# Fills, two factor products, four stores and three GpSimd steps moved between engines in a fused attention and feed-forward kernel

## The chip, the cores and the metric

One core of one Trainium2 chip. The metric is the device time of one execution in microseconds. The time before is the median of three runs.

## The reference

The inputs are q, k and v of 4 batches, 8 heads, 768 positions and 64 columns, and three arrays of a feed-forward layer. Attention comes first; every query sees the 8 first keys and the 96 last ones (abbreviated here):

```python
scores = scale * np.matmul(q, k.transpose(0, 1, 3, 2))
keep = is_global | is_local
dist = np.where(is_global & ~is_local, float(n_local), np.abs(rel))
scores = np.where(keep, scores - slopes[:, None, None] * dist, -1e9)
a = softmax(scores)                      # over the keys
x = (a @ v) as 3072 rows of 512
h = x @ w_in                             # 3072 x 1024
solu = h * softmax(h)                    # over the 1024
ln = (solu - mean(solu)) / sqrt(var(solu) + 1e-6) * g_ln
out = ln @ w_out                         # 3072 x 512, float32
```

## The kernel before, in words

**Tiling.** The program handles the batches one after the other, and within a batch four pairs of heads. For each pair it loads q and k (L477), casts them to 16 bits on VectorE, ScalarE or GpSimd (`x`, L264, L266, L268), turns them on TensorE (L741; for batch 3 by DMA, L776) and copies the result to `qT` and `kT`. Scores of a pair stand in two groups of key blocks (L892); ScalarE takes their exponential into `eb` (L900). In batch 0 the distance bias is added by a matmul (L878); in batches 1 to 3 `eb` is multiplied by a ready factor `fb` instead (L909, the "factor product": one instruction on VectorE, four quarters on GpSimd). Sums (L973), the logarithm (L989, L998), its spread to all rows (L1028), its exponential `rr` (L1037), the product with v (L1072, with a small VectorE read `tick`, L1082, between its halves) and the scaling to `xT` (L1097) end the attention of half a batch.

**The feed-forward part** has 24 row tiles of 128. A tile takes a first product (L1133), an exponential `ef` on ScalarE (L1140), VectorE's product `uu` (L1143), a sum of squares (L1150 or L1154), a turn of `uu` (L1169, from tile 5 on by DMA, L1159), small statistics (L1189 to L1198), a second product with the centred weights (L1215), the scaling `osb` (L1226, L1229) and a store (L1233). The first tile to be handled is tile 2.

**Weights.** `w_out` is multiplied by g (the weighting, L644 to L651, on three engines), TensorE forms the mean over the rows (L658), and VectorE subtracts it in eight steps (the centring, L662). The mean stays in one PSUM bank while the centring reads it; the first second product, that of tile 2, writes the same bank.

**The order.** Every piece of work is a numbered `step` with the engines that may do it. Three tables written into the program decide: `ORDER` is the order in which all steps are issued, so each engine and each queue executes its own in this order; `SLOTS` gives the buffers; `ENGS` the engine where a step has a choice. `WARM` names places in ORDER at which spare matmuls are put. An instruction waits only for what it needs, but everything behind it on its engine waits as well. SyncE issues nearly all DMAs; two stores at the end are issued by ScalarE.

**The steps that the change and the prediction touch:**

- 6, `c_slr` (L372 to L374): eight memsets of `slr`, which `constants_far` (L385) reads on VectorE. On GpSimd it stands between `c_spread` (L361) and a cast of v.
- 359 and 362: the factor products of batch 1, second group, pairs 0 and 1, both on VectorE. 359 stands between a cast of v and `uu` of tile 2 and reads the exponential of step 358, done at 25.52 us. 362 stands behind 350, the product of the first group's pair 1, ahead of an `xT` product, a copy, another `xT` product and the centring.
- on GpSimd from 27.5 us: casts of q of batch 1, pairs 2 and 3; one weighting step (159, two halves); casts of k, pairs 2 (300) and 3 (313); two casts of v; two kg steps; two weighting steps.
- 302 and 315: copies of the turned k of pairs 2 and 3, on ScalarE and on VectorE (L264, L266).
- 836, 824, 830 and 907: the stores of tiles 5, 3, 4 and 9. Their `osb` are written by VectorE (5, 3, 4) and ScalarE (9).
- 602, 51, 662 and 637 on GpSimd: the kg of batch 3, pair 0 (L523), its `vgz` (L515), the cast of its v of pair 2 and the cast of its k of pair 3 (L268). They stand behind 683, the factor product of batch 3, second group, pair 0.
- 519: the first scores of batch 2's second group. They write the bank pair that the first product of tile 4 used, which is free when `uu` of tile 4 has been formed.

Of the kernel before, what the change touches and what calls it, by code (L numbers as in the profile page):

```python
# [60 lines left out]
"""  # L61
SLOTS = """
# [10 lines left out]
"""  # L73
ENGS = """
# [1206 lines left out]
```

## Time and profile before

| what | value |
|---|---|
| median of three runs | 152.86 us (152.83 to 153.1) |
| the profiled execution | 152.65 us, its span 150.9 us |
| TensorE busy | 142.4 us, 94% |
| VectorE busy | 117.9 us, 78% |
| ScalarE busy | 122.1 us, 81% |
| GpSimd busy | 69.9 us, 46% |
| DMA queue of SyncE | 76120 packets, 97.5% of 16 engines' span |
| DMA queue of ScalarE | 288 packets, 0.9% |

The span is the time from the first to the last instruction of one profiled execution; 1.75 us of that execution's own time lie around it. Busy times of TensorE count pipelined matmuls with modelled ends, so small waits can hide in them. In the rows PE is TensorE, DVE VectorE, ACT ScalarE, POOL GpSimd and SP SyncE; L12 is line 12 of the program, and the lines named above are the lines of the rows. A row of a timeline gives the start in us from the span's start, the length in us, the engine, the line, the operation, out<-in with the shapes, and how many instructions are merged; in brackets stand the idle time of the engine before it and what ended it by the semaphores.

### The profile page before, as it was taken

Reading aid. Unit: us, or ns where it says so; the run is one execution under the profiler, and the core shown is the slowest. Engines: PE = TensorE matmul, PEld = TensorE weight load, DVE = VectorE, ACT = ScalarE, POOL = GpSimd, SP = SyncE. Lnnn points to the kernel's source line nnn. Section 1 sums busy time; section 2 is a strip of 40 time slices with the busy share of each in tenths; the row PEclk is TensorE's granted clock in tenths of the full one; section 3 lists DMA queues with packets and bytes.
Section 4 is the critical chain, followed back from the end, with each engine's and each line's share of the span. In section 5 each row is a group of like instructions: output and inputs, shape, how many; then the busy total and the mean of one; then the engine's idle time right before and its main releaser. Section 6 shows DMA issues by size and latency. Waiting matters only on the chain.

```text
span 150.9 us, 4802 instructions
## 1 busy us (share of the span) xinstructions
PE 142.4 (94%) x1870; PEld 76.7 (51%) x1870; DVE 117.9 (78%) x241; ACT 122.1 (81%) x209; POOL 69.9 (46%) x192
## 2 busy tenths in 40 slices
PE   5979799999998999999999999999999999999991
PEld 2536556466554566744454645444446644444450
DVE  6939897998999997989899966697785874898200
ACT  3949899899999789899997987978895776874641
POOL 6784447559899769735922240498130000110000
PEclk9999999999999999999999999999999999999999
DMA  4999999999999999999999999998999946488743
GB/s 140 367 307 342 300 382 337 362 337 401 309 295 182 247 323 220 240 216 250 241 160 235 260 161 260 162 221 159 223 212 260 216 125 128 81 245 208 231 152 139
DMA packets 76430, 36.35 MB, mean 241 GB/s; under 512 B 65456, under 2 KB 71928, under 8 KB 76408
## 3 DMA queue, kind: packets, MB, share of 16 engines
q1 hardware_dynamic: 76120, 35.54, 97.5%
q10 hardware_dynamic: 288, 0.52, 0.9%
q8 instruction: 14, 0.23, 0.6%
q14 instruction: 8, 0.07, 0.1%
HBM read 23.15 MB, written 6.29 MB: 195 GB/s over the span
## 4 chain that ended last, share of the span: by engine, by line
PE 72%; ACT 9%; DMA 7%; SPq 5%; DVE 4%; issue 1%; DVEq 0%; ACTq 0%
PE acc L1215 28%; PE acc L1133 23%; PE acc L1072 6%; DMA vt<-in_v_dram 4%; DMA x<-in_q_dram 3%; PE acc L892 3%; ACT eb L900 3%; PE acc L1028 3%; PE acc L973 2%; PE acc L741 2%; SPq L477 2%; ACT ef L1140 2%; DVE x L266 2%; PE acc L1062 1%; SPq L499 1%
## 5 line engine op out<-in xcount | busy, mean ns | idle before, releaser
L1215 PE MATMUL acc<-gw_out_sb,late 128*128 128x512 f16 (+1 forms) x200 | 44.3, 371 | 0.4 <-DMA vt<-in_v_dram 0.4
L1133 PE MATMUL acc<-w_in_sb,xT 128*128 128x512 f16 x192 | 44.7, 379 | 0.0
L1143 DVE SCALAR_TENSOR_TENSOR uu<-ef,acc 128x1024 f16<-128x1024 f16 x24 | 29.2, 1216 | 8.6 <-ACT ef L1140 8.4
L900 ACT ACTIVATE eb<-acc 128x896 f16<-128x896 f32 (+1 forms) x32 | 29.1, 955 | 1.5 <-PE acc L892 1.4
L1140 ACT ACTIVATE ef<-acc 128x1024 f16<-128x1024 f32 x24 | 24.7, 1030 | 6.5 <-PE acc L1133 6.5
L1215 PEld LDWEIGHTS <-late 128*128 128x128 f16 x200 | 18.9, 98 | 21.5 <-issue 1.3
L1133 PEld LDWEIGHTS <-xT 128*128 128x128 f16 x192 | 17.8, 98 | 21.4 <-issue 1.4
L268 POOL CAST x<-x 128x384 f16<-128x384 f32 (+1 forms) x32 | 17.9, 586 | 12.3 <-DMA x<-in_q_dram 6.2
L1097 DVE TENSOR_TENSOR xT<-acc,rr 128x384 f16<-128x384 f32 x32 | 16.3, 551 | 3.9 <-ACT rr L1037 1.5
L1072 PE MATMUL acc<-eb,v 64*64 64x160 f16 (+4 forms) x448 | 16.0, 221 | 0.6 <-DVE xT L1097 0.3
L1150 ACT ACTIVATE sqa<-uu 128x1024 f16<-128x1024 f16 x15 | 15.9, 1063 | 0.0
L909 POOL TENSOR_TENSOR eb<-eb,fb 128x240 f16<-128x240 f16 (+1 forms) x20 | 12.5, 656 | 6.1 <-ACT eb L900 6.1
L1072 PEld LDWEIGHTS <-v 64*64 64x64 f16 x448 | 12.9, 106 | 4.5 <-issue 3.4
L1037 ACT ACTIVATE rr<-acc 128x768 f32<-128x768 f32 x16 | 12.6, 811 | 2.8 <-PE acc L1028 1.9
L268 POOL CAST v<-v 128x384 f16<-128x384 f32 (+3 forms) x23 | 10.9, 492 | 7.2 <-DMA v<-in_v_dram 6.3
L909 DVE TENSOR_TENSOR eb<-eb,fb 128x896 f16<-128x896 f16 (+1 forms) x19 | 13.3, 727 | 1.1 <-ACT eb L900 1.1
L741 PE MATMUL acc<-ident,x 128*128 128x128 f16 x144 | 11.1, 220 | 1.5 <-ACT x L264 1.0
L892 PE MATMUL acc<-qT,kT 64*64 64x160 f16 (+2 forms) x384 | 11.8, 227 | 0.0
L1154 DVE SCALAR_TENSOR_TENSOR sqv<-uu 128x1024 f16<-128x1024 f16 x9 | 11.3, 1251 | 0.1
L741 PEld LDWEIGHTS <-x 128*128 128x128 f16 x144 | 8.5, 98 | 4.8 <-ACT x L264 1.4
L1226 ACT ACTIVATE x<-acc,rstd 128x512 f32<-128x512 f32 (+1 forms) x9 | 5.8, 640 | 6.2 <-PE acc L1215 6.2
L1062 PE MATMUL acc<-eg,vgz 64*64 64x384 f16 x64 | 10.7, 324 | 0.0
(120 smaller groups left out, 206.1 us busy)
## 6 DMA issues: line engine op xcount, KB each, us to landing
x<-in_q_dram SPq DMA_DIRECT2D x16, 384.0 KB, 5.8
x<-in_k_dram SPq DMA_DIRECT2D x16, 384.0 KB, 5.1
out_dram<-osb SPq DMA_DIRECT2D x12, 256.0 KB, 4.9
v<-in_v_dram SPq DMA_DIRECT2D x12, 192.0 KB, 4.5
out_dram<-x SPq DMA_DIRECT2D x9, 256.0 KB, 2.3
late<-in_moe_w_in_dram SPq DMA_DIRECT2D x4, 512.0 KB, 6.6
w_out<-in_moe_w_out_dram SPq DMA_DIRECT2D x4, 512.0 KB, 6.0
v<-in_v_dram SPq DMA_DIRECT2D x12, 160.0 KB, 4.7
```

The source lines that it names most:

```text
L268: nc.gpsimd.tensor_copy(out=out, in_=in_)
L741: nc.tensor.transpose(out=pt[:, ts(j, P)], in_=a[:, j, ts(pp, P)], identity=ident)
L892: nc.tensor.matmul(out=sc[o : o + 64, par, col : col + n], lhsT=kk[r, BLK * c : BLK * c + BLK], rhs=qq[r, g0 : g0 + n], start=fresh, stop= ...
L900: ex["fn"] = (lambda ex=ex, qk=qk, gw=gw: nc.scalar.activation(out=eb[at(qk, "eb")][:, :, 0:gw], in_=big(qk)[:, :, 0:gw], func=AF.Exp, sca ...
L909: (nc.gpsimd if fx["at"] == "POOL" else nc.vector).tensor_tensor(out=e[:, :, y], in0=e[:, :, y], in1=fb[:, p, :, y], op=ALU.mult)
L1072: nc.tensor.matmul(out=o_[64 * h : 64 * h + 64, gl : gl + m], lhsT=vv[r, v_at(vi, h, c), pair, :], rhs=view(eb[at(e_own[b, gi, pair], "eb" ...
L1097: nc.vector.tensor_tensor(out=xT[at(xt_own[b], "xT")][:, p, q0:q1], in0=one(av, d)[:, 0:w], in1=rr[at(re, "rr")][:, d, 0:w], op=ALU.mult)
L1133: nc.tensor.matmul(out=ph()[:, ts(fh, 512)], lhsT=xT[at(xt_own[b], "xT")][:, j, ts(t % NA, P)], rhs=w_in_sb[:, j, ts(fh, 512)], start=((j, ...
L1140: ex["fn"] = lambda g1=g1, t=t, ph=ph: nc.scalar.activation(out=ef[at(g1, "ef")], in_=ph(), func=AF.Exp, accum_out=s0[:, t : t + 1])
L1143: u["fn"] = lambda u=u, g1=g1, t=t, ph=ph: nc.vector.scalar_tensor_tensor(out=uu[at(u, "uu")], in0=ef[at(g1, "ef")], scalar=USC, in1=ph(), ...
L1150: nc.scalar.activation(out=sqs_["ACT"], in_=uu[at(u, "uu")], func=AF.Square, scale=float(D_FF) ** 0.5, accum_out=s2[:, t : t + 1])
L1215: nc.tensor.matmul(out=one(g2)[:, 0:wd], lhsT=uT[at(el_o, "uT")][:, c, :], rhs=gw_out_sb[:, c, sl_], start=(c == 0), stop=(c == NFC - 1))
```

## The change

It changes three lines of code and the four tables. The tables are long lists of numbers; what follows from them is this:

- `c_slr` runs on VectorE, behind the copy of q that ends at 8.46 us and ahead of the next cast.
- Step 359 runs on GpSimd, in four quarters, behind the cast of q of pair 3 and ahead of the weighting step 159.
- Step 362 stays on VectorE and stands behind the eight centring steps and `uu` of tile 5, ahead of a copy of q.
- Stores may now be issued by ScalarE for every tile; four are. 836 and 824 (tiles 5 and 3) stand behind the exponential `ef` of tile 6 and ahead of an `rr` exponential (L1037); 830 (tile 4) stands behind a sum of squares and ahead of an `osb`; 907 (tile 9) behind `rstd` (L1198) and ahead of an `osb`. They leave SyncE's list at four places, in front of loads and transposes.
- On GpSimd 602, 51 and 662, and with them 637, stand ahead of 683.

All else keeps its place on its engine: TensorE's list with the spare matmuls, SyncE's other DMAs, and all buffers are the same.

```diff
     def constants_slr():
         for h in range(H):
-            nc.gpsimd.memset(slr[:, h : h + 1], -slopes[h] * NL)
+            nc.vector.memset(slr[:, h : h + 1], -slopes[h] * NL)
...
-    slr_st = step("POOL", 270, -59000, [], constants_slr, name="c_slr")
+    slr_st = step("DVE", 560, -59000, [], constants_slr, name="c_slr")
...
-                        wd * 1.31, tg + 2500, [ou], eng=("SP",) if x < 20 else ("SP", "ACT"), name="store", iss=420)
+                        wd * 1.31, tg + 2500, [ou], eng=("SP", "ACT"), name="store", iss=420)
...
 ORDER = """
-126 86 12 11 271 2 13 17 16 10 15 66 14 18 0 20 73 36 3 75 7 1 4 88 68 69 89 22 53 55 56 90 8 70 38 79 81
+126 271 2 52 86 12 11 18 66 13 73 0 36 3 53 17 20 7 16 38 10 15 14 1 79 4 88 28 68 115 22 60 75 117 69 89
...
 WARM = """
-25:0:16 30:2:4 37:3:2 48:5:3 118:7:4
+34:0:16 43:2:4 49:3:2 59:5:3 126:7:4
```

## Rows read from the trace of the kernel before

**Rows 1.** Windows: us, busy us of PE, PEld, DVE, ACT, POOL, clock, DMA share, GB/s.

```profile
40.00:52.00 12.00, 11.53 (x109) 5.51 (x111) 12.00 (x20) 10.88 (x21) 11.04 (x23) 1.00 1.11 246
60.00:120.00 60.00, 60.00 (x875) 31.59 (x875) 49.17 (x91) 50.87 (x88) 25.29 (x58) 1.00 1.13 215
```

**Rows 2.** Timeline of TensorE around 50 us.

```profile
48.17 1.89 PE L1215 MATMUL acc<-gw_out_sb,late 128*128 128x512 f16 x8 [0.43 <-DMA vt<-in_v_dram]
...
51.92 0.22 PE L878 MATMUL acc<-bw,identb 64*64 64x64 f16 x2
```

**Rows 3.** Timeline of VectorE, 28 to 52 us.

```profile
28.04 0.92 DVE L909 TENSOR_TENSOR eb<-eb,fb 128x896 f16<-128x896 f16 x1
28.89 1.21 DVE L1143 SCALAR_TENSOR_TENSOR uu<-ef,acc 128x1024 f16<-128x1024 f16 x1
...
30.26 0.56 DVE L266 CAST x<-x 128x768 f16<-128x768 f32 x1 [0.15 <-DMA x<-in_q_dram]
...
35.30 0.96 DVE L266 COPY kT<-acc 128x768 f16<-128x768 f16 x1
...
39.84 1.49 DVE L909 TENSOR_TENSOR eb<-eb,fb 128x960 f16<-128x960 f16 x2
40.40 0.92 DVE L909 TENSOR_TENSOR eb<-eb,fb 128x896 f16<-128x896 f16 x1
41.25 0.54 DVE L1097 TENSOR_TENSOR xT<-acc,rr 128x384 f16<-128x384 f32 x1
...
42.78 5.34 DVE L662 SCALAR_TENSOR_TENSOR gw_out_sb<-w_out,g,acc 128x512 f16<-128x512 f32 x8
48.04 1.21 DVE L1143 SCALAR_TENSOR_TENSOR uu<-ef,acc 128x1024 f16<-128x1024 f16 x1
...
50.65 1.21 DVE L1143 SCALAR_TENSOR_TENSOR uu<-ef,acc 128x1024 f16<-128x1024 f16 x1
```

**Rows 4.** Timeline of VectorE, start of the kernel.

```profile
1.40 0.77 DVE L305 MEMSET sl<- 64x1 f32 x8
...
7.50 0.96 DVE L266 COPY qT<-acc 128x768 f16<-128x768 f16 x1
11.01 0.72 DVE L266 CAST x<-x 128x768 f16<-128x768 f32 x1 [2.55 <-DMA x<-in_q_dram]
```

**Rows 5.** Timeline of ScalarE, tile 2's exponential, its last part.

```profile
28.65 0.19 ACT L1140 ACTIVATION_READ_ACCUMULATOR ef<-acc 128x1 f32 x1
```

**Rows 6.** Timeline of GpSimd, casts, weighting and factor products.

```profile
28.90 0.96 POOL L268 CAST x<-x 128x384 f16<-128x384 f32 x2 [0.41 <-DMA x<-in_q_dram]
31.66 1.18 POOL L647 TENSOR_TENSOR gw_out_sb<-w_out,g 128x256 f16<-128x256 f32 x2 [1.80 <-DMA w_out<-in_moe_w_out_dram]
32.78 2.01 POOL L268 CAST x<-x 128x384 f16<-128x384 f32 x4
...
58.52 2.74 POOL L909 TENSOR_TENSOR eb<-eb,fb 128x240 f16<-128x240 f16 x4
...
96.54 2.31 POOL L909 TENSOR_TENSOR eb<-eb,fb 128x224 f16<-128x224 f16 x4 [5.89 <-ACT eb L900]
```

**Rows 7.** Timeline of VectorE, a cast and four factor products.

```profile
59.70 1.06 DVE L266 CAST x<-x 128x768 f16<-128x768 f32 x1
...
106.33 2.30 DVE L909 TENSOR_TENSOR eb<-eb,fb 128x896 f16<-128x896 f16 x4 [0.53 <-ACT eb L900]
```

**Rows 8.** Timeline of TensorE, the transposes of k of batch 1, pair 3.

```profile
34.42 0.77 PE L741 MATMUL acc<-ident,x 128*128 128x128 f16 x6
```

**Rows 9.** Timelines of ScalarE and of SyncE, a gap and two stores.

```profile
82.68 0.81 ACT L1037 ACTIVATE rr<-acc 128x768 f32<-128x768 f32 x1 [0.77 <-PE acc L1028]
...
143.37 0.37 ACTq L1233 DMA_DIRECT2D out_dram<-x  x1
...
81.59 1.40 SPq L1233 DMA_DIRECT2D out_dram<-osb  x1
```

**Rows 10.** Chain that ended last: start, us, what.

```profile
114.55 0.56 PE acc L973 x24
```

80 rows, old and new, of tables (ENGS, ORDER, SLOTS) are left out of this document.

## The prediction

> **What bounds the kernel now.** I read the windows by stage first. From 60 to 120 us TensorE is busy for 60.00 of 60 us; from 40 to 52 us it is VectorE that has no idle time (12.00 of 12), with TensorE at 11.53 [rows 1]. The granted clock is 1.00 in all of these stretches, so the clock is no part of the argument. What can be won therefore lies ahead of 52 us, and whatever delay TensorE still has at 52 us goes to the end unreduced, because nothing idles behind it.
>
> Next the timeline of TensorE around 50 us [rows 2]. The first output product (tile 2, L1215) starts at 48.17 us after 0.43 us of idle time; the bank that it writes is the one the centring reads, and VectorE's eight centring steps, begun at 42.78 us, end at 42.78 + 5.34 = 48.12 us [rows 3]. That is the wait the change aims at. But four starts later, at 51.92 us, the scores of batch 2 (L878) begin in the bank pair that VectorE's product `uu` of tile 4 gives back, and that product ends at 50.65 + 1.21 = 51.86 us [rows 2, 3]. So TensorE and VectorE arrive at 52 us together: a faster start at 48.17 us alone brings nothing unless tile 4's `uu` is earlier too. The reader is to see that VectorE's row of steps from 35 to 52 us is the path that decides, and its total work, not its order.
>
> **The change part by part.**
>
> *Fills of slopes to VectorE.* Eight memsets, as long there as the eight of `sl`, 0.77 us. They come behind the copy that ends at 7.50 + 0.96 = 8.46 us, and VectorE's next step starts at 11.01 us after 2.55 us of waiting for a load [rows 4]. They fit: cost nothing. If that load came 1.8 us earlier they would cost up to 0.77 us.
>
> *The product of batch 1, second group, pair 0, to GpSimd.* On VectorE it takes 0.92 us from 28.04 us. The next step there, `uu` of tile 2, starts at 28.89 us, but the exponential that it reads ends at 28.65 + 0.19 = 28.84 us, and the cast behind it waits until 30.26 us for a load [rows 3, 5]. So VectorE gains 0.05 us at most: it idles instead. GpSimd is free from 28.90 + 0.96 = 29.86 us and waits 1.80 us, until 31.66 us, for the output weights [rows 6]. Four quarters of this width cost 2.31 us there undisturbed; the product beginning at 58.52 us took 2.74 us, and beside it VectorE's cast of `x` took 1.06 us where the same cast took 0.56 us at 30.26 us [rows 3, 6, 7]. The new product has that very cast, at 30.26 us, beside it.
>
> The Trainium skill (SBUF — State Buffer, section SBUF: two separate sides) says that a GpSimd instruction and a VectorE one that needs the shared port pair exclude each other for the whole instruction. By it the cast would hold up GpSimd for its full 0.56 us, 2.87 us in all; the pair of lengthened rows agrees in kind.
>
> So GpSimd is through at 29.86 + 2.31 = 32.17 us or 29.86 + 2.74 = 32.60 us, 0.5 to 0.9 us behind the start of the weighting at 31.66 us. Behind it stand two weighting halves and then the casts of batch 1's keys, pairs 2 and 3. These take 2.01 us for four where two take 0.96 us, so about 0.1 us of waiting inside is swallowed. TensorE turns these keys at 34.42 us, and its six transposes take 0.77 us because it already waits for the second half of the last cast [rows 6, 8]; VectorE copies the result at 35.30 us [rows 3], first step of its unbroken row. Nothing covers this delay: the bounds are +0.3 us (part of it swallowed at each hand-over) and +0.9 us. The rows give 2.74 us for a product of 240 columns a quarter; for 224 columns 2.56 us, 0.7 us late, less the 0.1 us: I take **+0.6 us**.
>
> *The product of pair 1 behind the centring.* It goes from ahead of the centring (0.92 us at 40.40 us) to behind `uu` of tile 5 (48.04 us), ahead of tile 4's `uu` [rows 3]. The centring and the product at 48.17 us come earlier by its slot, 41.25 − 40.40 = 0.85 us (its successor, an `xT` product, starts at 41.25 us [rows 3]), but the work ahead of 51.86 us is the same. What can change is its length: four such products back to back take 2.30 us [rows 7], 0.57 each, so it loses up to 0.28 us if GpSimd is quiet at the new place, and nothing if GpSimd casts there too; its old neighbour could be lengthened by as much in its stead. Bounds −0.3 and +0.3 us; GpSimd has casts at both places, half of the gain: **−0.15 us**.
>
> *Four stores begun by ScalarE* (tiles 5 and 3 behind an exponential, 4 and 9 further on). An issue there took 0.37 us, at the end of the kernel. Two of them stand in the 0.77 us before the exponential of the spread logarithms at 82.68 us [rows 9]; 0.74 us fits. The other two are alone in front of waits. Cost nothing, as long as they are that short. SyncE's later loads and transposes move up by the slots left; TensorE waits for none of them there [rows 1], so no gain.
>
> *Three (with the last cast of keys: four) ready steps of GpSimd ahead of a product.* GpSimd idles 5.89 us before that product at 96.54 us [rows 6]. A kg step, two halves of `vgz` and two casts are under 4 us, so they fit. Should the cast of keys wait for its buffer, the product behind it waits with it; its readers, the sums at 114.55 us [rows 10], are 18 us later. Nothing either way.
>
> **Sum:** 0 − 0.05 + 0.6 − 0.15 + 0 + 0 = +0.4 us. The profiled execution took 152.65 us, 0.21 us below the median of the three runs, 152.86 us; so 152.65 + 0.4 = 153.05 us for such an execution and 152.86 + 0.4 = 153.26, say 153.3 us, for a median. 0.2% of this kernel is 0.31 us, about what a measurement can tell from no change; the forecast lies just beyond it.
>
> **The rivals.**
>
> *It evens out.* GpSimd is undisturbed (+0.3 us) and the moved product sheds its 0.28 us: 152.86 us, anything within 0.31 us. For it: the cast at 30.26 us overlaps only one quarter of four. Against it: the lengthened pair of rows. 0.29.
>
> *Faster: the wait at 48.17 us goes.* TensorE starts tile 2's product 0.43 us earlier, which counts from the point where tile 4's `uu` ends at least 0.43 us earlier too: the moved product alone at its new place (−0.28 us), its neighbour at 39.84 us not lengthened either, and GpSimd's new product hidden in the 1.80 us of waiting as far as the key casts' readers can see. Price −0.43 us: 152.4 us. For it: VectorE's products were lengthened twice before (0.92 us at 28.04 and 40.40 us [rows 3]) and one of the two leaves it. Against it: 2.31 us do not fit into 1.80 us. 0.23.
>
> *Slower by the stores.* SyncE's issue of the same kind took 1.40 us at 81.59 us, when the DMA engines were full [rows 9]. Should ScalarE be held as long, the two stores cost 2.8 − 0.77 = 2.0 us in front of 82.68 us, more than the later gaps of ScalarE return; TensorE's tiles behind wait for these exponentials, about +1.5 us, 154.4 us. Against it: ScalarE has a queue of its own that holds nothing. 0.04.
>
> **How the numbers follow.** Forecast (GpSimd's delay reaches 52 us) 0.44, evens out 0.29, faster 0.23, stores 0.04. Slower by over 0.2%: 0.44 + 0.04 = 0.48; within: 0.29; faster: 0.23. Of the forecast the bounds +0.9 and +0.3 − 0.3 give 152.9 to 154.1 us; the range 152.5 to 153.9 us leaves out the dearest tail, the stores and the lower half of the faster case. The forecast's own range is 153.1 to 153.9 us.
>
> **What would show it.** Right: on GpSimd the product at 29.9 us taking 2.3 to 2.9 us, the weighting behind it at 32.2 to 32.6 us, VectorE's copy of keys (35.30 us before) at 35.6 to 36.2 us; VectorE idle ahead of tile 2's `uu`; TensorE's first output product without its 0.43 us of waiting, and a new wait at the scores of batch 2 near 52.3 us; no idle TensorE behind. Wrong: the scores of batch 2 earlier than 51.9 us, or the weighting still at 31.7 us, or a stall of ScalarE at a store.

## The result and the profile after

| | kernel before | changed kernel | ratio, 95% interval |
|---|---|---|---|
| first measurement | 153.00 us (152.83 to 153.18) | 154.97 us (154.26 to 156.92) | 1.0104 [1.0062, 1.0147] |
| second measurement, another chip | 153.7 us | 156.19 us (155.27 to 158.76) | 1.0162 [1.0130, 1.0195] |

The forecast was 153.3 us, within 152.5 to 153.9 us: slower, as it came, but the loss is 1.0 to 1.6% where 0.3% was expected. Each set of runs has its own runs of the kernel before on the same chip; the chips of the later sets scatter more than the first. A ratio leaves disturbed executions out, so it isn't always that of the two medians.

The profile shown is that of the changed kernel in the second measurement: 155.27 us, span 153.4 us. In the kernels of the runs the tables are one to three lines longer, so here every line stands two higher: L1235 is the store, L911 the factor product, L880 the scores' first line.

Page of the changed kernel: the head, the DMA queues, and the costliest group.

```profile
span 153.4 us, 4804 instructions
...
PE 142.8 (93%) x1870; PEld 76.8 (50%) x1870; DVE 117.0 (76%) x248; ACT 122.4 (80%) x209; POOL 72.8 (47%) x188
...
q1 hardware_dynamic: 75544, 34.49, 95.0%
q10 hardware_dynamic: 864, 1.57, 2.9%
...
L1135 PE MATMUL acc<-w_in_sb,xT 128*128 128x512 f16 x192 | 44.4, 379 | 1.4 <-ACT osb L1228 1.4
```

TensorE's work is the same 142 us; what is new is 1.4 us of idle time before a first product, ended by ScalarE's `osb`. The stages show where (windows, columns as in [rows 1]).

```profile
40.00:52.00 12.00, 11.52 (x119) 5.85 (x117) 12.00 (x21) 11.70 (x21) 10.46 (x23) 1.00 0.98 228
60.00:90.00 30.00, 29.96 (x442) 16.42 (x440) 27.54 (x51) 27.47 (x48) 14.34 (x32) 1.00 1.17 216
90.00:100.00 10.00, 8.62 (x96) 4.29 (x94) 5.45 (x11) 7.27 (x14) 6.28 (x15) 1.00 1.21 219
```

From 60 to 120 us TensorE was never idle before [rows 1]; now it loses 1.38 us between 90 and 100 us. The clock is 1.00 throughout. The timelines of ScalarE, TensorE and SyncE give the cause.

```profile
88.29 0.69 ACT L1228 ACTIVATE osb<-acc,rstd 128x512 f32<-128x512 f32 x1 [0.51 <-PE acc L1217]
...
93.87 0.21 ACT L1200 ACTIVATE rstd<-vb 128x3 f32<-128x3 f32 x1
96.02 0.34 ACTq L1235 DMA_DIRECT2D out_dram<-osb  x1
96.48 0.69 ACT L1228 ACTIVATE osb<-acc,rstd 128x512 f32<-128x512 f32 x1 [2.40 <-DMA late<-uu]
...
97.22 1.89 PE L1135 MATMUL acc<-w_in_sb,xT 128*128 128x512 f16 x8 [1.38 <-ACT osb L1228]
...
82.21 3.36 SPq L778 DMA_TRANSPOSE qT<-x  x1
...
90.09 3.73 SPq L1161 DMA_TRANSPOSE late<-uu  x1
```

ScalarE has finished `rstd` at 94.08 us. Next in its list is the store of tile 9, whose `osb` (the row at 88.29 us) has been ready since 88.98 us. It begins only at 96.02 us, 1.94 us later, and its issue then takes 0.34 us. What ended the wait is a DMA of SyncE, the transpose of a `uu` begun at 90.09 us, with which the store has no data in common; by the trace it landed at 96.00 us. In this program all DMAs, of whichever queue, share eight completion semaphores in turn (the counters that tell that a transfer has landed; the trace has 143 DMAs on eight of them, 17 or 18 on each), and the program makes a DMA that comes to use one wait until the transfer that used it before has landed. The store and that transpose have the same one. Everything behind the store on ScalarE waits with it: `osb` of the next tile, whose PSUM bank TensorE's first product at 97.22 us needs. Of the 2.40 us of idle time in front of this `osb`, 0.94 us were there before, in a wait for TensorE:

```profile
93.94 0.69 ACT L1226 ACTIVATE osb<-acc,rstd 128x512 f32<-128x512 f32 x1 [0.94 <-PE acc L1215]
```

So the store adds about 1.5 us, and TensorE loses 1.38 us.

The other half of the loss lies earlier (VectorE, GpSimd and TensorE; to be held against [rows 2, 3, 6]).

```profile
30.23 2.62 POOL L911 TENSOR_TENSOR eb<-eb,fb 128x224 f16<-128x224 f16 x4
32.81 1.18 POOL L649 TENSOR_TENSOR gw_out_sb<-w_out,g 128x256 f16<-128x256 f32 x2
...
36.30 0.96 DVE L268 COPY kT<-acc 128x768 f16<-128x768 f16 x1 [0.70 <-PE acc L743]
...
43.49 5.34 DVE L664 SCALAR_TENSOR_TENSOR gw_out_sb<-w_out,g,acc 128x512 f16<-128x512 f32 x8
48.75 1.21 DVE L1145 SCALAR_TENSOR_TENSOR uu<-ef,acc 128x1024 f16<-128x1024 f16 x1
...
49.89 0.61 DVE L911 TENSOR_TENSOR eb<-eb,fb 128x896 f16<-128x896 f16 x1
...
51.82 1.21 DVE L1145 SCALAR_TENSOR_TENSOR uu<-ef,acc 128x1024 f16<-128x1024 f16 x1
...
48.88 1.89 PE L1217 MATMUL acc<-gw_out_sb,late 128*128 128x512 f16 x8 [0.41 <-DMA vt<-in_v_dram]
53.09 0.22 PE L880 MATMUL acc<-bw,identb 64*64 64x64 f16 x2 [0.31 <-DVE uu L1145]
```

By these times the copy of keys is 1.0 us late, `uu` of tile 4 and the scores of batch 2 1.2 us. About 0.4 us of that is not the change's: GpSimd's cast of q ahead of the product already ends at 30.27 us and not at 29.86 us, and in the profiles of the runs it ends anywhere between 29.8 and 31.3 us, with the product behind it or without. From that cast's end to the copy it is 6.03 us against 5.44 us. The first output product still waits (0.41 us; 0.43 us before), and the scores have a wait of 0.31 us that they didn't have.

### The profile page after: what moved, and what is told of

It is laid out like the page before. It is cut to its first block, busy times and chain, and to the rows that moved or that the text cites. A ratio compares the mean times of both kernels' runs of the same rounds, so it can differ in the third digit from the quotient of the medians.

```text
span 154.9 us, 4804 instructions
## 1 busy us (share of the span) xinstructions
PE 143.2 (92%) x1870; PEld 76.9 (50%) x1870; DVE 116.6 (75%) x248; ACT 122.1 (79%) x209; POOL 71.4 (46%) x188
## 4 chain that ended last, share of the span: by engine, by line
PE 55%; DVE 9%; DMA 4%; ACT 2%; issue 1%; ACTq 0%; DVEq 0%
PE acc L1215 24%; PE acc L1133 18%; DMA late<-uu 4%; PE acc L1072 4%; DVE gw_out_sb L662 3%; PE acc L892 2%; PE acc L973 2%; DVE xT L1097 2%; PE acc L1028 1%; PE acc L741 1%; DVE uu L1143 1%; PE acc L1062 1%; DVE sqv L1154 1%; DVE l L998 1%; PE acc L946 1%
## 5 line engine op out<-in xcount | busy, mean ns | idle before, releaser
L909 POOL TENSOR_TENSOR eb<-eb,fb 128x240 f16<-128x240 f16 (+1 forms) x24 | 15.2, 663 | 1.5 <-ACT eb L900 1.5
L1037 ACT ACTIVATE rr<-acc 128x768 f32<-128x768 f32 x16 | 12.6, 811 | 2.8 <-PE acc L1028 1.9
L909 DVE TENSOR_TENSOR eb<-eb,fb 128x896 f16<-128x896 f16 (+1 forms) x18 | 12.5, 714 | 0.8 <-ACT eb L900 0.8
```

The source lines that it names most:

```text
L909: (nc.gpsimd if fx["at"] == "POOL" else nc.vector).tensor_tensor(out=e[:, :, y], in0=e[:, :, y], in1=fb[:, p, :, y], op=ALU.mult)
```

## The experiments

Edits of the tables are shown as the lists of the engines they touch, by step numbers, with "..." for what is left out between. "Order only" is the base of most.

**Parts of the change: stores, the rest, and the interleaving.** The changed kernel again:

```diff
 (the changed kernel, nothing edited)
```

> The changed kernel once more, for a profile to set the others against. Theory A (the stores on ScalarE): ScalarE stands idle for about 2 us in front of the store of tile 9, waiting for an earlier transfer to land, and TensorE waits for 1 to 2 us at a first product behind it; 154.3 to 155.3 us. Theory B (the product on GpSimd): the scores of batch 2 start at 52.5 us or later where they started at 51.9 us; the same time. Theory C (the interleaving of the lists, which sets the semaphores): TensorE is already 0.5 us late at 26 us, as in the first profile of this kernel; the same time.

156.19 us, ratio 1.0162 [1.0130, 1.0195]: above the expected time. That chip's kernel before is above too, but the ratio is also larger than the first one. ScalarE's idle time (2.40 us) and the late scores (53.09 us) are both there.

The four stores back with SyncE:

```diff
-ScalarE: 841 836 824 537 ... 857 830 906 ... 862 907 876
+ScalarE: 841 537 ... 857 906 ... 862 876
-SyncE: 609 616 606 858 635 642 844 632 625 619 851 612
+SyncE: 609 836 616 824 606 858 635 642 907 844 632 625 619 851 830 612
```

> The changed kernel with the four stores back in SyncE's list, all else as changed. Theory A: nearly all of the loss goes, 153.0 to 153.6 us (what is left is the 0.4 us of the forecast), and TensorE has no wait over 0.5 us between 90 and 100 us. Theory B: only the part behind 90 us goes, 154.0 to 154.6 us. Theory C: little goes, about 154.5 us.

154.52 us, 1.0064 [1.0037, 1.0091]. Only the stores on ScalarE:

```diff
-VectorE: 90 6 62 ... 193 773 ... 350 265 ... 815 362 445
+VectorE: 90 62 ... 193 359 773 ... 350 362 265 ... 815 445
-GpSimd: 9 119 ... 320 359 159 ... 602 51 662 637 683 628 615 641
+GpSimd: 9 6 119 ... 320 159 ... 683 637 602 628 662 615 51 641
```

> The changed kernel with the fills, both factor products and the GpSimd steps back at their old engines and places; the four stores stay on ScalarE. Theory A: 154.0 to 154.8 us, with ScalarE idle for about 2 us in front of the store of tile 9. Theory B: 153.0 to 153.3 us. Theory C: 153.6 us, and the scores of batch 2 start late although GpSimd has no product there.

154.93 us, 1.0065 [1.0031, 1.0098], with 2.20 us of idle time of ScalarE and 1.18 us of TensorE. "Order only" takes both edits:

```diff
-ScalarE: 841 836 824 537 ... 857 830 906 ... 862 907 876
+ScalarE: 841 537 ... 857 906 ... 862 876
-SyncE: 609 616 606 858 635 642 844 632 625 619 851 612
+SyncE: 609 836 616 824 606 858 635 642 907 844 632 625 619 851 830 612
-VectorE: 90 6 62 ... 193 773 ... 350 265 ... 815 362 445
+VectorE: 90 62 ... 193 359 773 ... 350 362 265 ... 815 445
-GpSimd: 9 119 ... 320 359 159 ... 602 51 662 637 683 628 615 641
+GpSimd: 9 6 119 ... 320 159 ... 683 637 602 628 662 615 51 641
```

> Every step on its old engine and every engine's own list as before; only the interleaving of the lists is that of the changed kernel. Theories A and B: 153.0 us, within 0.3 us of the kernel before. Theory C: 153.5 us or more, with TensorE late at 26 us.

153.23 us, 0.9986 [0.9959, 1.0013]. So theory C falls, and neither A nor B is the whole: the stores cost 0.65%, the rest 0.64%, about 1.0 us each. Every kernel below is "order only" plus one part, unless said otherwise.

**The two factor products.** The product of pair 0 alone:

```diff
-VectorE: 193 359 773
+VectorE: 193 773
-GpSimd: 320 159
+GpSimd: 320 359 159
```

> Of the change only the product of batch 1, second group, pair 0 on GpSimd, in front of the weighting. Theory A (the whole loss beside the stores is this product, through the casts of keys): the weighting starts 1.0 to 1.2 us later than in the kernel with only the interleaving changed (31.84 us there), VectorE's copy of the keys of pair 3 and its uu of tile 4 0.9 to 1.0 us later, and the time is 0.5 to 0.9 us above the kernel before. Theory B (the product alone is swallowed, and it is the other product, moved behind the centring, that costs): the scores of batch 2 within 0.3 us of their old time, and the time of the kernel before.

154.22 us, 1.0053 [1.0015, 1.0090]: as far as the intervals tell, it is the cost of "the rest" (0.64%). GpSimd and VectorE in this kernel, then in "order only" (lines one higher than before in both):

```profile
29.77 2.66 POOL L910 TENSOR_TENSOR eb<-eb,fb 128x224 f16<-128x224 f16 x4
32.39 1.19 POOL L648 TENSOR_TENSOR gw_out_sb<-w_out,g 128x256 f16<-128x256 f32 x2
...
39.77 1.35 POOL L269 CAST x<-x 128x384 f16<-128x384 f32 x2
41.09 5.61 POOL L910 TENSOR_TENSOR eb<-eb,fb 128x240 f16<-128x240 f16 x8
...
35.89 0.96 DVE L267 COPY kT<-acc 128x768 f16<-128x768 f16 x1 [0.71 <-PE acc L742]
...
40.67 1.93 DVE L910 TENSOR_TENSOR eb<-eb,fb 128x960 f16<-128x960 f16 x2
42.53 0.54 DVE L1098 TENSOR_TENSOR xT<-acc,rr 128x384 f16<-128x384 f32 x1
...
51.86 1.21 DVE L1144 SCALAR_TENSOR_TENSOR uu<-ef,acc 128x1024 f16<-128x1024 f16 x1
```

```profile
40.15 1.75 POOL L269 CAST x<-x 128x384 f16<-128x384 f32 x2 [0.71 <-DMA x<-in_k_dram]
41.86 4.82 POOL L910 TENSOR_TENSOR eb<-eb,fb 128x240 f16<-128x240 f16 x8
...
35.51 0.96 DVE L267 COPY kT<-acc 128x768 f16<-128x768 f16 x1 [0.21 <-PE acc L742]
...
40.04 1.49 DVE L910 TENSOR_TENSOR eb<-eb,fb 128x960 f16<-128x960 f16 x2
...
50.87 1.21 DVE L1144 SCALAR_TENSOR_TENSOR uu<-ef,acc 128x1024 f16<-128x1024 f16 x1
```

The weighting starts at 32.39 us, inside the predicted 32.2 to 32.6 us. From GpSimd's cast of q to the copy of keys it takes 35.89 − 29.81 = 6.08 us, against 35.30 − 29.86 = 5.44 us before: the predicted 0.6 us ("order only" has 35.51 − 29.86 = 5.65 us, so against that kernel it is 0.4 us). Theory A had expected more here, 1.0 to 1.2 us at the weighting and 0.9 to 1.0 us at the copy. But from the copy to `uu` of tile 4 it takes 15.97 us where "order only" takes 15.36 us. VectorE's two products now run beside GpSimd's two (41.09 us, 5.61 us for eight quarters; in "order only" these begin at 41.86 us and take 4.82 us), and both sides are lengthened, VectorE's by 1.93 − 1.49 = 0.44 us. GpSimd's two begin earlier, not later: the cast of keys ahead of them, which in "order only" waits 0.71 us for its load, comes later here and finds it landed, while VectorE's two come 0.6 us later. The delay grows on its way, to 1.0 us at `uu` of tile 4 as theory A has it; TensorE waits 0.73 us at 43.13 us, for the `xT` product behind VectorE's two.

Not all of this growth has to be the product's. In "only the stores", where the product is on VectorE, GpSimd's two also begin early, and VectorE's two are lengthened too (lines two higher):

```profile
41.31 5.19 POOL L911 TENSOR_TENSOR eb<-eb,fb 128x240 f16<-128x240 f16 x8
...
40.02 1.79 DVE L911 TENSOR_TENSOR eb<-eb,fb 128x960 f16<-128x960 f16 x2
```

From the copy to `uu` of tile 4 the kernels with both products on VectorE at their old places take 15.0 to 15.7 us. How much of the growth the product causes, and how much hangs on when that load of keys lands, isn't shown.

The product of pair 1 alone:

```diff
-VectorE: 350 362 265 ... 815 445
+VectorE: 350 265 ... 815 362 445
```

> Of the change only the product of pair 1 moved behind the centring and uu of tile 5. Theory A: the centring ends 0.5 to 0.9 us earlier (47.66 us in the kernel with only the interleaving changed; here 46.8 to 47.8), uu of tile 4 no earlier than it by more than 0.3 us, and the time is that of the kernel before within 0.3 us. Theory B: uu of tile 4 ends 0.3 us or more later than 52.08 us and the time is 0.4 us or more above the kernel before.

153.34 us, 0.9971 [0.9935, 1.0007]. Rows of TensorE:

```profile
47.64 1.89 PE L1216 MATMUL acc<-gw_out_sb,late 128*128 128x512 f16 x8
...
51.85 0.22 PE L879 MATMUL acc<-bw,identb 64*64 64x64 f16 x2 [0.32 <-DVE uu L1144]
```

The wait in front of the first output product is gone, and a new one of 0.32 us stands four starts later at the scores of batch 2: `uu` of tile 4 starts at 50.59 us, 0.28 us earlier than in "order only". Whether the time falls isn't settled, since the interval reaches 1. One place further, behind that `uu`:

```diff
-VectorE: 350 362 265 ... 815 445 373 807 365
+VectorE: 350 265 ... 815 445 373 807 362 365
```

> The product of pair 1 moved one place further than the change does, behind uu of tile 4 as well, all else as before. If that uu is what TensorE waits for at 51.85 us (0.32 us at the scores of batch 2), then the wait goes too: uu of tile 4 ends at about 51.2 us, the scores start at 51.5 us, and the time is 0.993 to 0.997 of the kernel before. If VectorE's total work up to the sums at 54.3 us decides: the wait moves there and the time is that of the kernel with the product behind the centring alone.

153.60 us, 0.9993 [0.9955, 1.0031]: no gain over the kernel before is shown, and the expected 0.993 to 0.997 did not come, though the interval reaches 0.9955. No profile of it is read here, so where the wait went stays open.

**The store of tile 9.** Alone on ScalarE:

```diff
-SyncE: 642 907 844
+SyncE: 642 844
-ScalarE: 862 876
+ScalarE: 862 907 876
```

> Of the change only the store of tile 9 on ScalarE; the other three stores stay with SyncE. Theory A (its wait for an earlier transfer to land is the stores' whole cost): ScalarE stands idle for 2 us or more in front of it, TensorE for about 1.2 us behind, and the time is 0.8 to 1.2 us above the kernel before. Theory B (the four together crowd ScalarE or the transfers): no such idle time, and at most 0.3 us above the kernel before.

154.34 us, 1.0035 [1.0003, 1.0067], with 2.14 us of idle time of ScalarE around the store. The idle time is theory A's; the cost, 0.5 us, lies under its 0.8 to 1.2 us, but the interval reaches 1.0 us. Here, in "only the stores" and in the changed kernel the store begins 0.02 us after the transpose on its semaphore has landed. The next kernel has all four stores and one transfer more, from q to a tile that nothing reads:

```diff
+    turn_x = sb.tile([1, 16], FP32, name="turn_x")
...
             s["fn"]()
+        if s["i"] == 851:
+            nc.sync.dma_start(out=turn_x, in_=q[0, 0, 0:1, 0:16])
```

> The kernel with only the four stores changed, and one transfer of 64 bytes more, begun by SyncE behind the transpose that follows tile 9's store, so that its only effect on that store is to pass it on to the next of the eight completion semaphores: there the transfer ahead of it is the store of tile 4, which was begun at 87 us, and not the transpose that lands at 95 us. Theory A (the semaphore's earlier user must land first): the idle time of 2.2 us in front of the store goes to under 0.5 us, TensorE's wait of 1.2 us at 96 us goes with it, and the time is within 0.4 us of the kernel before. Theory B (transfers begun by ScalarE stand still because the DMA engines are full): the idle time stays at about 2 us, and the time at 1.0 us above the kernel before.

155.22 us, 1.0107 [1.0061, 1.0154]. Half of theory A came true. The wait at the store of tile 9 is gone, by nothing but another semaphore: it begins at 95.88 us, and the transpose that it would else have followed landed only at 97.93 us. But SyncE began the load of q ahead of these stores at 82.39 us (81.21 us in the changed kernel), and the store of tile 4 now waited for that load to land, with 1.34 us of waiting on TensorE behind it (ScalarE's rows, then TensorE's):

```profile
87.42 0.83 ACT L267 CAST x<-x 128x768 f16<-128x768 f32 x1 [1.59 <-DMA x<-in_k_dram]
...
90.10 0.39 ACTq L1236 DMA_DIRECT2D out_dram<-osb  x1
90.61 0.69 ACT L1229 ACTIVATE osb<-acc,rstd 128x512 f32<-128x512 f32 x1 [1.30 <-DMA x<-in_q_dram]
...
95.88 0.34 ACTq L1236 DMA_DIRECT2D out_dram<-osb  x1
96.52 0.69 ACT L1229 ACTIVATE osb<-acc,rstd 128x512 f32<-128x512 f32 x1 [0.44 <-PE acc L1218]
...
91.35 2.75 PE L1136 MATMUL acc<-w_in_sb,xT 128*128 128x512 f16 x12 [1.34 <-ACT osb L1229]
```

That load landed at 90.02 us; in the changed kernel it had landed at 87.70 us, 0.08 us before the store. ScalarE came to the store late as well: the cast ahead of it waited 1.59 us for a load of k; in the kernel before it doesn't wait. So which store waits depends on which transfer it follows and how late that one is. The store of tile 9 alone on ScalarE, but four steps later:

```diff
-SyncE: 642 907 844
+SyncE: 642 844
-ScalarE: 862 876 926 682 931 670
+ScalarE: 862 876 926 682 931 907 670
```

> Of the change only the store of tile 9 on ScalarE, but four steps later in ScalarE's list (behind the exponential of the tile that follows), where the transfer ahead of it on its semaphore is a transpose begun at about 93.5 us. Theory A: the store is reached at about 97.5 to 98 us, when that transpose has landed or is about to; under 0.6 us of idle time in front of it, no wait over 0.5 us on TensorE at 96 us, and the time of the kernel before within 0.3 us. Theory B (a store on ScalarE costs wherever it stands): idle time of about 2 us there and 0.5 us or more above the kernel before.

153.66 us, 1.0015 [0.9981, 1.0048]; the store begins at 97.14 us without waiting; the transpose on its semaphore had landed at 95.24 us. As theory A has it.

**The other three stores.** Tiles 5, 3 and 4 on ScalarE:

```diff
-SyncE: 609 836 616 824 606 ... 851 830 612
+SyncE: 609 616 606 ... 851 612
-ScalarE: 841 537 ... 857 906
+ScalarE: 841 836 824 537 ... 857 830 906
```

> Of the change only the stores of tiles 5, 3 and 4 on ScalarE; tile 9's stays with SyncE. By the assignment of the semaphores the store of tile 4 then comes behind a load that has long landed. Theory A (a store on ScalarE costs what the transfer ahead of it on its semaphore still needs to land, and else nothing): no idle time over 0.4 us in front of these three beyond what TensorE's results cause, no wait of TensorE over 0.3 us at 80 to 100 us, and the time of the kernel before within 0.3 us. Theory B (the issues themselves crowd ScalarE): 0.3 us or more above the kernel before.

154.23 us, 1.0057 [1.0027, 1.0087], without a wait of ScalarE in front of them, but for 0.74 us in which a cast ahead of tile 4's store waits for its load of k: against theory A. The two first alone:

```diff
-SyncE: 609 836 616 824 606
+SyncE: 609 616 606
-ScalarE: 841 537
+ScalarE: 841 836 824 537
```

> Of the change only the stores of tiles 5 and 3 on ScalarE. Theory A (only waits of ScalarE in front of a store cost): the time of the kernel before within 0.3 us. Theory C (the two stores, let in at the same time as SyncE's loads, hold up SyncE's list): the transpose behind them takes 3.4 us or more to issue instead of 1.3 to 1.7, SyncE's list reaches the loads of v at 105 to 108 us 0.5 us or more later than where it began it, TensorE waits for a transposed q at about 107.8 us, and the time is 0.5 us or more above the kernel before.

153.88 us, 0.9999 [0.9958, 1.0040]. The transpose behind them does take 3.65 us to issue, but no loss is seen, and TensorE doesn't wait for a transposed q at 107.8 us. The interval reaches 0.6 us, so theory C's 0.5 us is made unlikely for these two and not excluded. The store of tile 4 alone:

```diff
-SyncE: 851 830 612
+SyncE: 851 612
-ScalarE: 857 906
+ScalarE: 857 830 906
```

> Of the change only the store of tile 4 on ScalarE, where no transfer is ahead of it on its semaphore. Theories A and C: the time of the kernel before within 0.3 us. If this store carries the cost of the three: 0.5 us or more above it.

153.91 us, 1.0054 [1.0021, 1.0087]: this one carries it, against theories A and C. On ScalarE it begins at 85.22 us, from SyncE at 98.07 us. The same store on ScalarE at its old time:

```diff
-SyncE: 851 830 612
+SyncE: 851 612
-ScalarE: 931 670
+ScalarE: 931 830 670
```

> Of the change only the store of tile 4 on ScalarE, and there ten steps later than the change has it, at about 97 us, the time at which SyncE began it before (98.07 us in the kernel with only the interleaving changed). Theory D (its early transfer, at 85 to 87 us among SyncE's loads, delays what SyncE does behind): the time of the kernel before within 0.3 us, and no wait of TensorE for a cast of v over 0.3 us at 115 us. If the store costs by standing on ScalarE or by the turn of the semaphores: 1.003 to 1.008 of the kernel before, as where it stands early (1.0054).

153.85 us, 0.9994 [0.9957, 1.0032]. So, by the ratios of two chips, it does not cost by standing on ScalarE but by being early. Two things change with that: when its transfer runs, and the turn of the semaphores, which the early store shifts by one for the DMAs between the two places; no run tells them apart. How the time is lost, only single profiles tell: with the early store TensorE waits at 115 us for GpSimd's cast of v, whose load comes late, and with the late one it doesn't.

```profile
114.99 0.25 PE L1074 MATMUL acc<-eb,v 64*64 64x160 f16 x1 [0.41 <-POOL v L270]
```

SyncE reaches these loads at 106.80 us, against 105.39 us in "order only"; but it reaches them at 106.74 us with the late store, and among kernels with SyncE's list as before that time goes from 104.96 to 108.11 us. One of those, with all four stores on SyncE, has such a wait too (0.28 us at 114.86 us; the first kernel of "Two versions" below). So this link isn't shown.

**The fills and the GpSimd steps:**

```diff
-VectorE: 90 62
+VectorE: 90 6 62
-GpSimd: 9 6 119 ... 683 637 602 628 662 615 51 641
+GpSimd: 9 119 ... 602 51 662 637 683 628 615 641
```

> Of the change only the fills on VectorE and the four GpSimd steps ahead of the product. All theories: the time of the kernel before within 0.3 us; the product of batch 3 that they are moved ahead of starts up to 4 us later than at 96.5 us if the cast of keys among them waits, and TensorE does not notice. Against them all: 1.003 or more.

154.52 us, 1.0005 [0.9961, 1.0049]: no cost is seen; the interval is 0.7 us wide to either side. GpSimd:

```profile
98.54 0.96 POOL L269 CAST x<-x 128x384 f16<-128x384 f32 x2 [4.51 <-DMA qT<-x]
99.46 4.02 POOL L910 TENSOR_TENSOR eb<-eb,fb 128x224 f16<-128x224 f16 x4
```

The product takes 4.02 us here, and 2.31 us before.

**Two versions.** The changed kernel without the product on GpSimd and without stores on ScalarE:

```diff
-VectorE: 193 773
+VectorE: 193 359 773
-GpSimd: 320 359 159
+GpSimd: 320 159
-ScalarE: 841 836 824 537 ... 857 830 906 ... 862 907 876
+ScalarE: 841 537 ... 857 906 ... 862 876
-SyncE: 609 616 606 858 635 642 844 632 625 619 851 612
+SyncE: 609 836 616 824 606 858 635 642 907 844 632 625 619 851 830 612
```

> The changed kernel without its two costs: the product of pair 0 back on VectorE, the four stores back with SyncE; the fills, the product behind the centring and the GpSimd steps stay as changed. If the costs are these two alone: 152.4 to 153.0 us where the kernel before has 153.0, the same as the kernel with only the product behind the centring (0.997 of the kernel before). If the fills or the GpSimd steps cost too: 153.3 us or more.

153.70 us, 0.9972 [0.9938, 1.0005]: the ratio of the kernel with only the product of pair 1 moved (0.9971), as expected if the costs are these two alone. And the changed kernel with its two costs mended rather than undone:

```diff
-VectorE: 193 773
+VectorE: 193 359 773
-GpSimd: 320 359 159
+GpSimd: 320 159
-ScalarE: 862 907 876 926 682 931 670 912
+ScalarE: 862 876 926 682 931 907 670 912
```

> The changed kernel with two repairs: the product of pair 0 back on VectorE, and the store of tile 9 still on ScalarE but four steps later in its list. Theory A: no idle time over 0.6 us in front of any store except by chance at tile 4's, and the time of the kernel without that product and without stores on ScalarE, 0.994 to 1.000 of the kernel before. Theory C or a cost of stores on ScalarE as such: 1.002 or more.

154.18 us, 1.0042 [1.0003, 1.0081]: against theory A. The store of tile 4 is still early, and the later store of tile 9 gave up its buffer later; ScalarE's next `osb` in that buffer waits for it to land (0.82 us in the kernel with this store alone), and TensorE 0.89 us behind it:

```profile
96.83 0.34 ACTq L1235 DMA_DIRECT2D out_dram<-osb  x1
...
100.78 0.69 ACT L1228 ACTIVATE osb<-acc,rstd 128x512 f32<-128x512 f32 x1 [1.98 <-DMA out_dram<-osb]
```

Two kernels that leave out the product and the stores and keep the move behind the centring came out at 0.997, faster than the changed kernel; that they beat the kernel before isn't settled, since both intervals just reach 1.

## Why the prediction was right and wrong

**What bounds the kernel: right.** A delay of `uu` of tile 4 of 1.0 us (product of pair 0 alone) came out as 0.53%, 0.8 us of 153.7 us. And a faster start at 48 us is not won by itself: in the kernel with the product of pair 1 moved, of the 0.43 us of waiting that went there 0.32 us reappeared at the scores of batch 2, as the text said of it.

**Fills: right.** In the changed kernel the eight memsets take 0.17 us at 8.58 us, less than the 0.77 us assumed, and VectorE still waits 2.32 us for a load behind them.

**The product to GpSimd: the mechanism right, the term perhaps too small.** Its own sum is 2.56 us from 29.86 us, which is 0.76 us late and less the 0.1 us 0.66 us, written down as 0.6 us. The doubtful step is the one that carries the copy's delay unchanged to `uu` of tile 4 ("I take +0.6 us"). Against "order only" the delay was 0.4 us at the copy of keys (0.6 us against the kernel before) and 1.0 us at `uu`, where VectorE's two products had met GpSimd's two, 1.49 us grown to 1.93 us. The lengthening of neighbours was used for the new product's own place and not for the work pushed along by it. By the time alone, 0.8 us with an interval from 0.2 to 1.4 us, 0.6 us isn't refuted. The Trainium skill (SBUF — State Buffer, section SBUF: two separate sides) says that the port pair goes to the one engine or the other for a whole instruction; that both sides grew here (GpSimd's eight quarters from 4.82 to 5.61 us) agrees with it, though a shared rate would lengthen both as well.

**The product behind the centring: right in kind.** −0.15 us was taken from bounds of ±0.3 us. `uu` of tile 4 came 0.28 us earlier, the time 0.45 us by its ratio, with an interval that reaches from −1.0 to +0.1 us. In the changed kernel the centring ended at 48.83 us, later than before, so the 0.43 us at the first output product did not go: that sign was wrong, by the first product's delay. The same delay settles the faster rival, which needed GpSimd's product to fit into 1.80 us, and the rival by which it evens out, which needed 2.31 us; it took 2.62 us.

**The stores: wrong, and the largest miss.** This is the step that failed: the four stores were put at nothing and cost 0.65%, about 1.0 us. "Cost nothing, as long as they are that short" priced the issue, and it was that short (0.34 to 0.38 us). Two things were not priced: what an issue must wait for ahead of it (1.7 to 1.9 us of ScalarE at tile 9's store, 1.1 to 1.4 us of TensorE behind it), and when the store is begun (0.5% at tile 4's, by a way that stays open). The sentence on [rows 9] looked for the danger in front of the exponential at 82.68 us; no run shows a cost of the two stores there. The text did name "a stall of ScalarE at a store" as a sign of being wrong, and it came. The rival that stores hold ScalarE had the right engine and, with 154.4 us, the nearest time of all cases, but a chance of 0.04 and another mechanism: a longer issue, at those two stores. "ScalarE has a queue of its own that holds nothing" was its counterargument, and it misled: the queue is its own, the completion semaphores aren't. The Trainium skill (DMA: Bandwidth & Descriptors, section Anatomy of one DMA — SWDGE (gpsimd) path) says that DMA engines wait for no semaphore and that such a wait is the issuing sequencer's, before it sends the transfer off; the section is about transfers begun by GpSimd, and the 1.94 us of ScalarE agree with it. By this rule the question at each moved store would have been which semaphore it waits for.

"SyncE's later loads and transposes move up by the slots left" was wrong for the stores of tiles 5 and 3, though it entered the sum with nothing. The next transpose took the time back: 3.36 us to issue at 82.21 us in the changed kernel, 1.60 us in the profile before and 1.27 us in "order only".

**GpSimd's steps: right.** The cast of keys did wait, 4.51 us, the product behind it was 2.9 us later than [rows 6], and no change of the time was seen.

**The sum.** Forecast +0.4 us. By the parts: product +0.8, moved product −0.45, stores +1.0, the others 0, +1.35 us in all, with some 0.5 us of uncertainty each by their intervals; measured 1.6 us (1.04% of 153.0) and 2.5 us (1.62%) on the two chips. The stores (0.0, 0.5 and 0.35% alone) come to 0.65% together, [0.31, 0.98], so within their intervals they may add or not. Why the second chip lost more wasn't tried.

## What to carry to other kernels

When a compute engine is given a transfer to start, price three things and not only the issue: what the issue waits for (the earlier user of its semaphore, which may be another queue's slow transfer), what stands behind it on that engine, and what the transfer meets if it now starts earlier. When a step moves between two engines that lengthen each other's work (here VectorE and GpSimd), follow its delay to the end of the row: the work that it pushes along meets other neighbours than before. A wait that a reordering removes is worth only what the next engine to arrive leaves of it (here 0.32 of 0.43 us came back four starts later).

## What the runs showed of the hardware

A store of ScalarE stood 1.7 to 1.9 us for a transfer of SyncE that it shares only a semaphore with, and began 0.02 us after that transfer had landed; the wait is one that the program holds. A 64-byte transfer elsewhere in the list, by shifting the turn of the semaphores, was enough to remove it. With the DMA engines full (DMA share 1.17 between 60 and 90 us), two stores taken off SyncE's list freed no time there: the transpose behind the stores of tiles 5 and 3 took 3.2 to 4.3 us to issue in every kernel with these two on ScalarE, and 1.3 to 1.7 us in every kernel with them on SyncE. The Trainium skill (DMA: Bandwidth & Descriptors, section Issuing engines are not separate DMA queues) says that starting transfers on several engines only saves the time of starting them; here not even that was saved.
